# Softmax and V product of each pair of heads moved ahead of the next pair's key transposes

## Chip, cores and metric

The kernel runs on one core of a Trainium2 chip. The metric is device time in microseconds (us), the median of several executions. Before the change it is 446.15 us, the median of three (444.69 to 447.6). The profiled execution took 449.3 us, and its span from first to last instruction is 447.5 us.

## What is computed

One decoding step of a transformer block: batch 8, one new token, width 1024. Attention has 32 query heads on 4 key/value heads, a cache of 8192 keys, heads of width 128. A ReGLU block with 3584 hidden units follows, and both blocks take shift, scale and gate from a conditioning vector.

```python
mod = (_silu(c) @ w_mod)            # six parts: sa, ca, ga, sb, cb, gb
h = _layernorm(x) * (1 + ca) + sa
q = (h @ wq).reshape(B, Sq, Hq, Dh)          # 8, 1, 32, 128
scores = einsum('bhqd,bhkd->bhqk', q, k) * Dh ** (-0.5)   # 8192 keys
p = softmax(scores)
o = einsum('bhqk,bhkd->bhqd', p, v)
x = x + ga * (o @ wo)
h = _layernorm(x) * (1 + cb) + sb
x = x + gb * (relu(h @ W_gate) * (h @ W_up)) @ W_down
```

Nearly all bytes are the two caches: 8 batches x 4 key/value heads x 8192 x 128 x 2 bytes, 67 MB each. With the weights the profile counts 185.6 MB read from the chip's memory.

## The kernel before

The 32 (batch, key/value head) items are taken two at a time, so the attention loop runs over `M = 16` pairs m (L495). A pair needs one 4 MB key load and one 4 MB value load. Everything that is streamed goes through one ring in the on-chip memory, `arena`: nine slots of 8192 bf16 per partition. A key or value load fills two slots, so in the steady state four loads fit: K(m+2) overwrites K(m), and V(m+2) overwrites V(m) (because K(4) no longer fits at the end and wraps to the start).

All loads are issued by one engine, SyncE (SP), in one order: K(0), V(0), K(1), V(1), ..., then Wo, gate, up and down (L223 to L259). SyncE waits before each one until the last reader of the bytes it overwrites is through, and a load that waits holds back all later ones. The readers are the eight key transposes of the pair (`kt_part`, L423, on VectorE), and its 32 V products (`pv`, L477, on TensorE). After the attention the ring goes on with the weights: the second half of gate (gate 1) overwrites the first half of Wo.

Work on the compute engines stands in the order in which it is written; semaphores are planned from reads and writes (`Prog.plan`). For each pair:

- `kt_part(m, e8)`, e8 = 0..7: VectorE transposes an eighth of the keys, as 32-bit words, into a ring of six buffers `kt`.
- `qk_part(m, e8)`: four matmuls on TensorE (L434) for each eighth. The first four eighths go to one bank of PSUM, the other four to a second.
- `rowmax(m, h)`: VectorE takes the negated maximum of a bank (L441). `spread` joins the two on VectorE (L445) and spreads them over the partitions with a matmul (L447).
- `headmax`: two small VectorE operations (L452, L455) give the bias of the exponential.
- `expo`: ScalarE takes the exponential of both banks (L461), with the row sums.
- `p_turn`: two VectorE transposes of the probabilities (L468).
- `pv`: 32 matmuls (L477) that sum into bank 5.
- `fold`: four VectorE operations out of bank 5 (L484, L487), then a small matmul (L490).
- `make_qpad(m+2)`: GpSimd places the queries of a later pair (L416).

The order before is a software pipeline: the key work of pair m carries the softmax of pair m-1. After eighth 0 come `rowmax(m-1, 1)` and `spread(m-1)`, after eighth 1 `headmax` and `expo`, after eighth 3 `p_turn`, after eighth 4 `pv`, after eighth 7 `fold`, all of pair m-1. The last pair's softmax follows the loop by itself.

Of the kernel before, what the change touches and what calls it, by code (L numbers as in the profile page):

```python
# [132 lines left out]
def bass_adaLN_cond__gqa_block_cached__glu_gated_reglu__decode_kernel(nc, A_x, A_k_cache, A_v_cache, A_wq, A_wo, B_x, B_W_gate, B_W_up, B_W_down, c, w_mod, out):  # L133
# [18 lines left out]
    with ExitStack() as es:  # L152
# [29 lines left out]
        M = N // 2  # L182
# [24 lines left out]
        def R(t, lo=0, hi=1):  # L207
            return (t, lo, hi)

        def bank(b, n=1):  # L210
            return ("ps", b, b + n)

        def slot_r(lo, hi):
            return ("arena", lo, hi)
# [197 lines left out]
        def make_qpad(m):  # L412
            if m >= M:
                return
            for Q in range(4):
                P.op("pool", lambda e, n=2 * m + Q // 2, Q=Q: e.tensor_copy(  # L416
                    qpad[32 * Q:32 * Q + 32, m % 2, :, 24 + 32 * Q:32 + 32 * Q], qR[32 * Q:32 * Q + 32, :, n, :]),
                     reads=[R("qR", 0, 8)], writes=[R("qpad", m % 2, m % 2 + 1)])

        def kt_part(m, e8):  # L420
            lo = place["k", m] + e8 * QE
            to = (8 * m + e8) % 6 * QE
            P.op("dve", lambda e: e.transpose(ktb[:, to:to + QE].bitcast(dt.uint32), arena[:, lo:lo + QE].bitcast(dt.uint32)),  # L423
                 reads=[slot_r(lo, lo + QE)], writes=[R("kt", to, to + QE)])

        def qk_part(m, e8):
            to = (8 * m + e8) % 6 * QE
            i = e8 % 4
            b = 2 * (m % 2) + e8 // 4
            kv = ktb[:, to:to + QE].rearrange("p (c t k r) -> p c t k r", t=2, k=32, r=2)  # L430
            fns = []
            for t in range(2):
                for r in range(2):
                    fns.append(lambda e, t=t, r=r: e.matmul(  # L434
                        ps[:, b, :].rearrange("p (c k) -> p c k", k=32), qpad[:, m % 2, t * 2 + r, 24 - 8 * i:152 - 8 * i],
                        kv[:, :, t, :, r], start=(i == 0 and t == 0 and r == 0), stop=(i == 3 and t == 1 and r == 1)))
            P.op("pe", fns, reads=[R("kt", to, to + QE), R("qpad", m % 2, m % 2 + 1)], writes=[bank(b)])

        def rowmax(m, h):
            b = 2 * (m % 2) + h  # L440
            P.op("dve", lambda e: e.tensor_reduce(negm[:, h:h + 1], ps[:, b, :], AX.X, ALU.max, negate=True),  # L441
                 reads=[bank(b)], writes=[R("negm", h, h + 1)])

        def spread(m):
            P.op("dve", lambda e: e.tensor_tensor(out=negm[:, 2:3], in0=negm[:, 0:1], in1=negm[:, 1:2], op=ALU.min),  # L445
                 reads=[R("negm", 0, 2)], writes=[R("negm", 2, 3)])
            P.op("pe", lambda e: e.matmul(ps[:, 4, 0:128], negm[:, 2:3].to_broadcast([128, 128]), identf[:],  # L447
                                         start=True, stop=True), reads=[R("negm", 2, 3), R("identf")], writes=[bank(4)])

        def headmax(m):  # L450
            z = m % 2
            P.op("dve", lambda e: e.tensor_reduce(mj[:].rearrange("p (g j) -> p g j", g=2),  # L452
                                                  ps[:, 4, 0:128].rearrange("p (g m j) -> p g j m", g=2, j=J), AX.X, ALU.min),
                 reads=[bank(4)], writes=[R("mj")])
            P.op("dve", lambda e: e.scalar_tensor_tensor(out=mjt[:], in0=mj[:], scalar=1.0, in1=jms[:], op0=ALU.mult,  # L455
                                                         op1=ALU.mult, accum_out=bias[:, z:z + 1]),
                 reads=[R("mj"), R("jms")], writes=[R("mjt"), R("bias", z, z + 1)])

        def expo(m):
            z = m % 2  # L460
            P.op("act", lambda e: e.activation(prb[:], ps[:, 2 * z:2 * z + 2, :].rearrange("p h n -> p (h n)"), ACT.Exp,  # L461
                                               bias=bias[:, z:z + 1], scale=scale, accum_out=lall[:, m:m + 1]),
                 reads=[bank(2 * z, 2), R("bias", z, z + 1)], writes=[R("prb"), R("lall", m, m + 1)])

        def p_turn(m):
            z = m % 2
            for g in range(2):
                P.op("dve", lambda e, g=g: e.transpose(pT[64 * g:64 * g + 64, z, :, g, :], prb[64 * g:64 * g + 64, :]),  # L468
                     reads=[R("prb"), R("pT", z, z + 1)], writes=[R("pT", z, z + 1)])

        def pv(m):
            z = m % 2
            lo = place["v", m]
            vv = arena[:, lo:lo + 2 * SLOT].rearrange("p (h i c d) -> p h c i d", h=2, i=4, d=Dh)
            fns = []
            for t in range(32):
                fns.append(lambda e, t=t: e.matmul(  # L477
                    ps[64 * (t % 2):64 * (t % 2) + 64, 5, :].rearrange("p (i d) -> p i d", d=Dh),
                    pT[:, z, t].rearrange("p g x -> p (g x)"), vv[:, t // 16, t % 16], start=(t < 2), stop=(t >= 30),
                    tile_position=(0, 64 * (t % 2))))  # L480
            P.op("pe", fns, reads=[slot_r(lo, lo + 2 * SLOT), R("pT", z, z + 1)], writes=[bank(5)])

        def fold(m):
            P.op("dve", lambda e: e.tensor_scalar(out=om[:], in0=ps[:, 5, 0:Dh], scalar1=im[:, 0:1], scalar2=None, op0=ALU.mult),  # L484
                 reads=[bank(5), R("im")], writes=[R("om")])
            for i in range(1, 4):
                P.op("dve", lambda e, i=i: e.scalar_tensor_tensor(  # L487
                    out=om[:], in0=ps[:, 5, Dh * i:Dh * i + Dh], scalar=im[:, i:i + 1], in1=om[:], op0=ALU.mult, op1=ALU.add),
                     reads=[bank(5), R("im"), R("om")], writes=[R("om")])
            P.op("pe", lambda e: e.matmul(ps[:, 6, 16 * m:16 * m + 16], om[:], jmp[:].rearrange("p g j -> p (g j)"),  # L490
                                         start=True, stop=True), reads=[R("om"), R("jmp")], writes=[bank(6)])

# [2 lines left out]
        for m in range(M):  # L495
            for e8 in range(8):
                kt_part(m, e8)
                qk_part(m, e8)
                if m >= 1:
                    if e8 == 0:  # L500
                        rowmax(m - 1, 1)
                        spread(m - 1)
                    elif e8 == 1:
                        headmax(m - 1)
                        expo(m - 1)
                    elif e8 == 3:
                        p_turn(m - 1)
                    elif e8 == 4:
                        pv(m - 1)
                    elif e8 == 7:  # L510
                        fold(m - 1)
                if e8 == 5:
                    rowmax(m, 0)
            make_qpad(m + 2)
        rowmax(M - 1, 1)
        spread(M - 1)
        headmax(M - 1)
        expo(M - 1)
        p_turn(M - 1)
        pv(M - 1)  # L520
        fold(M - 1)


        P.op("dve", lambda e: e.tensor_tensor(out=lx[:], in0=lall[:, :, None].to_broadcast([128, M, 2 * J]),
# [127 lines left out]
```

## Time and profile before

| | |
|---|---|
| Median of three | 446.15 us (444.69 to 447.6) |
| Span of the profiled execution | 447.5 us |
| TensorE matmul busy | 267.8 us, 60% |
| VectorE busy | 262.7 us, 59% |
| ScalarE busy | 28.8 us, 6% |
| Main DMA queue, share of 16 engines' span | 97.7% |
| Read from memory | 185.63 MB, 415 GB/s over the span |
| 128 key transposes (L423) | 1224 ns each |
| 32 probability transposes (L468) | 1220 ns each |
| V products, 32 of a pair (L477) | 3.64 to 6.36 us a pair |
| Key landings that VectorE waits for | 55.9 us in 16 waits |

A page of this kind divides the span into 40 slices and gives each engine's busy share there, the clock that TensorE was granted, and the rate of the DMA engines. A window view does the same for any stretch of time. The chain view follows the end of the kernel back through what each step waited for. The timeline lists instructions in order of start, with the idle time before each and what ended it.

A compute engine at 60% and a DMA queue at 98% mean that the bytes are the first limit. What the order of the compute instructions can still change is when a slot of the ring comes free, and so whether the DMA engines have anything to fetch.

### The profile page before, as it was taken

The numbers are of one execution on the slowest core, as the hardware profiler recorded it, in microseconds if no ns is written. First come the engines' busy times: TensorE is split into PE (matmuls) and PEld (weight loads), VectorE is DVE, ScalarE is ACT, GpSimd is POOL, SyncE is SP. The second block draws the span as 40 slices with busy tenths as digits, with TensorE's granted clock in tenths as the row PEclk, the third lists the DMA queues.
The fourth block names the chain that finished last, engine by engine and source line by source line (L and its number), as shares of the span: only waits on it lengthen the run. The fifth ranks groups of instructions, "written<-read, shape, count | busy, mean of one in ns | idle before, by whom it ended". The sixth has DMA issues, their size and how long they took to land.

```text
span 447.5 us, 4025 instructions
## 1 busy us (share of the span) xinstructions
PE 267.8 (60%) x1690; PEld 114.4 (26%) x1690; DVE 262.7 (59%) x371; ACT 28.8 (6%) x48; POOL 19.9 (4%) x77
## 2 busy tenths in 40 slices
PE   0244335565687756586777757566777758535435
PEld 0111011132223323232323313222323323224212
DVE  0503054679596967869586866949596866353020
ACT  0200001101011010101011010101011010110000
POOL 6000010000000000000000000000000000000000
PEclk9986559598969989689888988998889988668855
DMA  8999999999999999999999999999899999999995
GB/s 348 415 435 425 447 434 429 428 431 436 429 431 404 435 451 422 425 414 428 425 432 387 428 423 390 425 425 438 363 442 377 439 425 420 440 418 396 419 427 212
DMA packets 7554, 185.90 MB, mean 415 GB/s; under 512 B 912, under 2 KB 1008, under 8 KB 1264
## 3 DMA queue, kind: packets, MB, share of 16 engines
q1 hardware_dynamic: 7504, 185.64, 97.7%
q8 instruction: 13, 0.21, 0.2%
q14 instruction: 5, 0.04, 0.0%
q10 hardware_dynamic: 32, 0.01, 0.0%
HBM read 185.63 MB, written 0.02 MB: 415 GB/s over the span
## 4 chain that ended last, share of the span: by engine, by line
DMA 45%; PE 25%; DVE 24%; issue 5%; ACT 1%; SPq 0%; POOL 0%; DVEq 0%; ACTq 0%; POOLq 0%
DMA arena<-in_A_k_cache_dram 37%; DVE kt L423 12%; PE ps L477 11%; PE ps L434 8%; DVE pT L468 6%; DMA arena<-in_B_W_down_dram 6%; DMA c_r<-in_c_dram 2%; PE ps L562 1%; PE ps L347 1%; PE ps L583 1%; DVE negm L441 1%; DVE mj L452 1%; PE ps L447 1%; DVE mjt L455 0%; DVE kt L552 0%
## 5 line engine op out<-in xcount | busy, mean ns | idle before, releaser
L434 PE MATMUL ps<-kt,qpad 128*128 128x512 bf16 x512 | 148.1, 430 | 105.1 <-DVE kt L423 61.8
L423 DVE STREAM_TRANSPOSE kt<-arena 128x1024 uint32<-128x1024 uint32 x128 | 152.8, 1224 | 56.3 <-DMA arena<-in_A_k_cache_dram 55.9
L434 PEld LDWEIGHTS ps<-kt,qpad 128*128 128x128 bf16 x512 | 47.4, 105 | 189.1 <-DVE kt L423 89.1
L477 PE MATMUL ps<-arena,pT 128*64 128x512 bf16 x512 | 72.5, 447 | 4.5 <-DVE pT L468 4.5
L477 PEld LDWEIGHTS ps<-arena,pT 128*64 128x64 bf16 x512 | 32.6, 128 | 44.8 <-issue 28.6
L468 DVE STREAM_TRANSPOSE pT<-prb 64x1024 bf16<-64x1024 bf16 x32 | 39.0, 1220 | 1.8 <-ACT prb L461 1.3
L461 ACT ACTIVATE prb<-ps,bias 128x1024 bf16<-128x1024 f32 x16 | 17.8, 1113 | 289.2 <-DVE mjt L455 289.2
L416 POOL COPY qpad<-qR 32x32 bf16<-32x32 bf16 x64 | 13.0, 203 | 321.8 <-PE ps L434 269.2
L484 DVE TENSOR_SCALAR om<-ps,im 128x128 f32<-128x128 f32 x16 | 5.6, 351 | 32.1 <-PE ps L477 32.1
L441 DVE TENSOR_REDUCE negm<-ps 128x1 f32<-128x512 f32 x32 | 20.9, 653 | 1.2 <-PE ps L434 1.2
L487 DVE SCALAR_TENSOR_TENSOR om<-ps,im,om 128x128 f32<-128x128 f32 x48 | 16.8, 351 | 1.7
L583 PE MATMUL ps<-arena,hT 128*32 128x448 bf16 x128 | 9.3, 457 | 10.1 <-DMA arena<-in_B_W_up_dram 6.8
L370 PE MATMUL ps<-arena,hT 128*32 128x512 bf16 x64 | 6.7, 566 | 12.2 <-DMA arena<-in_A_wq_dram 9.3
L347 PE MATMUL ps<-arena,hT 128*32 128x512 bf16 x96 | 9.7, 574 | 5.7 <-DMA arena<-in_w_mod_dram 5.7
L316 PE MATMUL ps<-st,sel 128*128 128x1 f32 x4 | 1.0, 311 | 19.6 <-DVE st L315 19.6
L601 PE MATMUL ps<-arena,kt 128*32 128x256 bf16 x112 | 6.9, 416 | 7.4 <-DMA arena<-in_B_W_down_dram 7.3
L590 DVE TENSOR_TENSOR kt<-ps,kt 128x448 bf16<-128x448 f32 x2 | 1.2, 620 | 17.3 <-PE ps L583 17.3
L354 DVE COPY mod<-ps 128x512 f32<-128x512 f32 x2 | 1.3, 670 | 14.7 <-PE ps L347 14.7
L380 DVE CAST kt<-ps 128x512 bf16<-128x512 f32 x1 | 0.7, 691 | 15.4 <-PE ps L370 15.4
L447 PEld LDWEIGHTS ps<-identf,negm 128*128 128x128 f32 x32 | 8.2, 266 | 5.3 <-DVE negm L445 2.3
L447 PE MATMUL ps<-identf,negm 128*128 128x128 f32 x32 | 8.4, 356 | 0.9 <-DVE negm L445 0.9
L288 DVE TENSOR_SCALAR lt<-lt 128x256 f32<-128x256 f32 x1 | 0.3, 293 | 13.3 <-ACT lt L287 13.3
(77 smaller groups left out, 94.9 us busy)
## 6 DMA issues: line engine op xcount, KB each, us to landing
arena<-in_A_k_cache_dram SPq DMA_DIRECT2D x16, 4096.0 KB, 24.3
arena<-in_A_v_cache_dram SPq DMA_DIRECT2D x16, 4096.0 KB, 14.8
arena<-in_w_mod_dram SPq DMA_DIRECT2D x4, 3072.0 KB, 14.7
arena<-in_A_wq_dram SPq DMA_DIRECT2D x4, 2048.0 KB, 29.6
arena<-in_A_wo_dram SPq DMA_DIRECT2D x2, 4096.0 KB, 25.0
arena<-in_B_W_gate_dram SPq DMA_DIRECT2D x2, 3584.0 KB
arena<-in_B_W_up_dram SPq DMA_DIRECT2D x2, 3584.0 KB
arena<-in_B_W_down_dram SPq DMA_DIRECT2D x1, 3584.0 KB
```

Of the source, the lines that this page charges most:

```text
L347: fns.append(lambda e, w=w, pr=pr, j=j, kk=kk: e.matmul(ps[32 * j:32 * j + 32, pr, :], hT[:, kk, :], w[:, 2 * pr:2 * pr + 2, j, :], start= ...
L416: P.op("pool", lambda e, n=2 * m + Q // 2, Q=Q: e.tensor_copy(qpad[32 * Q:32 * Q + 32, m % 2, :, 24 + 32 * Q:32 + 32 * Q], qR[32 * Q:32 * ...
L423: P.op("dve", lambda e: e.transpose(ktb[:, to:to + QE].bitcast(dt.uint32), arena[:, lo:lo + QE].bitcast(dt.uint32)), reads=[slot_r(lo, lo ...
L434: fns.append(lambda e, t=t, r=r: e.matmul(ps[:, b, :].rearrange("p (c k) -> p c k", k=32), qpad[:, m % 2, t * 2 + r, 24 - 8 * i:152 - 8 * ...
L441: P.op("dve", lambda e: e.tensor_reduce(negm[:, h:h + 1], ps[:, b, :], AX.X, ALU.max, negate=True), reads=[bank(b)], writes=[R("negm", h, ...
L447: P.op("pe", lambda e: e.matmul(ps[:, 4, 0:128], negm[:, 2:3].to_broadcast([128, 128]), identf[:], start=True, stop=True), reads=[R("negm" ...
L461: P.op("act", lambda e: e.activation(prb[:], ps[:, 2 * z:2 * z + 2, :].rearrange("p h n -> p (h n)"), ACT.Exp, bias=bias[:, z:z + 1], scal ...
L468: P.op("dve", lambda e, g=g: e.transpose(pT[64 * g:64 * g + 64, z, :, g, :], prb[64 * g:64 * g + 64, :]), reads=[R("prb"), R("pT", z, z + ...
L477: fns.append(lambda e, t=t: e.matmul(ps[64 * (t % 2):64 * (t % 2) + 64, 5, :].rearrange("p (i d) -> p i d", d=Dh), pT[:, z, t].rearrange(" ...
L487: P.op("dve", lambda e, i=i: e.scalar_tensor_tensor(out=om[:], in0=ps[:, 5, Dh * i:Dh * i + Dh], scalar=im[:, i:i + 1], in1=om[:], op0=ALU ...
L583: fns.append(lambda e, w=w, r=kk - r0, kk=kk, h=h, j=j, b0=b0: e.matmul(ps[32 * j:32 * j + 32, b0 + h, 0:H], hT[:, kk, :], w[:, r, j, h, : ...
L601: fns.append(lambda e, w=w, r=k - r0, k=k, j=j: e.matmul(ps[32 * j:32 * j + 32, 4, 0:256], hmT[:, k, :], w[:, r, j, :], start=(k == 0), st ...
```

## The change

The softmax of a pair no longer rides in the next pair's key work. After the eight eighths of pair m come its `rowmax(m, 1)`, `spread`, `headmax`, `expo`, `p_turn` and `pv`, and only then the first key transpose of pair m+1. The purpose is to have each pair's value slots read, and so released, before the next pair starts. `fold` of the pair before is placed where VectorE would otherwise wait for the last scores, and its matmul is split off as `fold_pe`, behind `spread`. No operation is added or removed, and the instructions themselves stay as they are.

```diff
@@ -487,6 +487,8 @@
                 P.op("dve", lambda e, i=i: e.scalar_tensor_tensor(
                     out=om[:], in0=ps[:, 5, Dh * i:Dh * i + Dh], scalar=im[:, i:i + 1], in1=om[:], op0=ALU.mult, op1=ALU.add),
                      reads=[bank(5), R("im"), R("om")], writes=[R("om")])
+
+        def fold_pe(m):
             P.op("pe", lambda e: e.matmul(ps[:, 6, 16 * m:16 * m + 16], om[:], jmp[:].rearrange("p g j -> p (g j)"),
                                          start=True, stop=True), reads=[R("om"), R("jmp")], writes=[bank(6)])
 
@@ -496,29 +498,21 @@
             for e8 in range(8):
                 kt_part(m, e8)
                 qk_part(m, e8)
-                if m >= 1:
-                    if e8 == 0:
-                        rowmax(m - 1, 1)
-                        spread(m - 1)
-                    elif e8 == 1:
-                        headmax(m - 1)
-                        expo(m - 1)
-                    elif e8 == 3:
-                        p_turn(m - 1)
-                    elif e8 == 4:
-                        pv(m - 1)
-                    elif e8 == 7:
-                        fold(m - 1)
                 if e8 == 5:
                     rowmax(m, 0)
             make_qpad(m + 2)
-        rowmax(M - 1, 1)
-        spread(M - 1)
-        headmax(M - 1)
-        expo(M - 1)
-        p_turn(M - 1)
-        pv(M - 1)
+            if m >= 1:
+                fold(m - 1)
+            rowmax(m, 1)
+            spread(m)
+            if m >= 1:
+                fold_pe(m - 1)
+            headmax(m)
+            expo(m)
+            p_turn(m)
+            pv(m)
         fold(M - 1)
+        fold_pe(M - 1)
```

## The prediction

> **What bounds the kernel now.** I read the page first: the slices of the DMA, then the chain.
>
> ```profile
> DMA  8999999999999999999999999999899999999995
> GB/s 348 415 435 425 447 434 429 428 431 436 429 431 404 435 451 422 425 414 428 425 432 387 428 423 390 425 425 438 363 442 377 439 425 420 440 418 396 419 427 212
> DMA 45%; PE 25%; DVE 24%; issue 5%; ACT 1%; SPq 0%; POOL 0%; DVEq 0%; ACTq 0%; POOLq 0%
> ```
>
> The DMA engines count as busy from start to end, so the bytes are the limit. But the rate isn't even: from the twenty-second slice on, some slices fall to 387, 390, 363, 377. The chain, less than half DMA, says that compute has a say in the loads. So I asked for the rate by stage, and for single microseconds around a dip (columns: stretch, its length, busy us of PE, PEld, DVE, ACT and POOL, granted clock, DMA share, GB/s).
>
> ```profile
> 62.50:160.00 97.50, 63.60 (x304) 25.72 (x304) 69.02 (x89) 6.10 (x9) 4.05 (x20) 0.85 1.00 428
> 160.00:200.00 40.00, 28.44 (x136) 11.84 (x136) 29.73 (x41) 2.41 (x4) 1.47 (x8) 0.83 1.01 432
> 200.00:240.00 40.00, 28.43 (x136) 11.82 (x136) 29.71 (x41) 2.41 (x4) 1.78 (x9) 0.87 0.99 418
> 240.00:280.00 40.00, 28.08 (x136) 11.91 (x136) 29.60 (x40) 2.41 (x4) 0.81 (x4) 0.87 0.97 410
> 280.00:360.00 80.00, 54.72 (x273) 22.66 (x273) 59.28 (x80) 4.82 (x8) 3.25 (x16) 0.89 0.98 416
> 361.60:441.00 79.40, 43.74 (x482) 22.87 (x482) 32.40 (x50) 5.47 (x9) 0.00 (x0) 0.71 0.99 419
> 317.00:318.00 1.00, 1.00 (x11) 0.38 (x8) 0.00 (x0) 0.00 (x0) 0.00 (x0) 1.00 0.46 197
> 318.00:319.00 1.00, 1.00 (x7) 0.46 (x6) 0.85 (x3) 0.00 (x0) 0.00 (x0) 1.00 0.08 33
> ```
>
> Undisturbed, the stream runs at 428 to 432 GB/s; later it runs at 415, and at 318 us it nearly stops. What it waited for stands in the waits of SyncE's queue and in the timelines around another dip.
>
> ```profile
> SPq L235 <- PE ps L477: 248.8, 13, 21.9
> ```
>
> ```profile
> 271.93 5.33 PE L477 MATMUL ps<-arena,pT 128*64 128x512 bf16 x32
> ```
>
> ```profile
> 277.30 0.33 SPq L235 DMA_DIRECT2D arena<-in_A_v_cache_dram  x1
> 277.67 0.43 SPq L235 DMA_DIRECT2D arena<-in_A_k_cache_dram  x1
> 280.17 1.25 DVE L423 STREAM_TRANSPOSE kt<-arena 128x1024 uint32<-128x1024 uint32 x1 [1.35 <-DMA arena<-in_A_k_cache_dram]
> ```
>
> SyncE stands behind the V products (L477). When they end at 277.26, V and K are issued together, and the previous K load, the last one in flight, lands only 2.9 us later. [...] So the queue holds under 1 us of data when it is refilled, or none: it runs by a hair, and dry whenever the V products are late.
>
> How late they are follows the pair's key landing T. With V products of 3.64 us the issue comes at T + 14.7 (landing at 239.85, issue at 254.59); with 5.33 us at T + 16.5 (260.76 to 277.30, 301.53 to 318.07, 322.42 to 338.90). The key landings are 19.4 to 21.4 us apart, 19.9 on average (62.69 to 361.61 over 15).
>
> [...] V products take 3.64 us at full clock and 6.36 in the tail at a clock near 0.5.
>
> **The change, part by part.** Nothing is removed or added; the same 128 transposes, 1024 large matmuls and 16 exponentials run. What moves:
>
> *Exposed softmax.* Pair 15 has no next pair to ride in, so the tail of before already shows the new order:
>
> ```profile
> 380.09 0.69 DVE L441 TENSOR_REDUCE negm<-ps 128x1 f32<-128x512 f32 x1 [1.19 <-PE ps L434]
> 381.03 0.49 PE L447 MATMUL ps<-identf,negm 128*128 128x128 f32 x2 [0.85 <-DVE negm L445]
> 382.10 1.11 ACT L461 ACTIVATE prb<-ps,bias 128x1024 bf16<-128x1024 f32 x1 [15.69 <-DVE mjt L455]
> 383.34 2.51 DVE L468 STREAM_TRANSPOSE pT<-prb 64x1024 bf16<-64x1024 bf16 x2 [1.27 <-ACT prb L461]
> 386.00 6.36 PE L477 MATMUL ps<-arena,pT 128*64 128x512 bf16 x32 [4.48 <-DVE pT L468]
> 392.40 0.35 DVE L484 TENSOR_SCALAR om<-ps,im 128x128 f32<-128x128 f32 x1 [6.54 <-PE ps L477]
> ```
>
> From the second rowmax to the end of the probability transposes: 380.09 to 385.85, 5.76 us, of which VectorE is idle about 2 us (spread and exponential). These 2 us are the added waits; queued behind them are the next pair's key transposes, and TensorE waits for those. From a key landing the VectorE path is: six transposes 6.88 (timeline at 62.69), first rowmax 0.65, two more transposes 2.37, fold 1.49 (which covers the wait for the last scores, 1.04 us at full clock), then 5.76: 17.15 us. The keys come every 19.5 us at 430 GB/s (8.39 MB). VectorE still ends 2.4 us before the next landing: the added waits lie beside the transfer and cost nothing.
>
> *TensorE.* The V products now stand ahead of the next pair's scores. Its first rowmax needs four eighths of scores. Counted from the end of the probability transposes: V products done at 0.15 + 5.33 = 5.5, and 16 score matmuls back to back take 3.7 (12 take 2.78 at 254.48), so 9.2. VectorE reaches that rowmax at 2.4 + 6.88 = 9.3. Even; no stall. If keys were always there, the period would be 9.2 + 0.65 + 2.37 + 1.49 + 5.76 = 19.5, as long as the transfer. With 3.64 us of V products it is 17.8; with 6.36 us and the first four scores at half clock (1.86 us, as at 221.03) 11.2 + 10.3 = 21.5. That last value is the unknown. One gap of some 4 us per pair remains on TensorE instead of two, and the scores keep it busy after it; I take 5.33.
>
> *The release.* The key slots are read at T + 6.88 + 0.65 + 2.37 = T + 9.9, and K(m+2) may be issued then. V products end at T + 17.15 + 0.15 + 5.33 = T + 22.6, and V(m+2) follows. At that moment the queue holds the rest of V(m+1), which lands at T + 29.3 (6.7 us), and all of K(m+2) (9.75 us): 16 us of data where it was under 1. Even half-clock V products can't empty it.
>
> *What it brings.* From 200 to 360 us the rate rises from 415 (418, 410, 416 weighted) to 430: 160 x (1 - 415/430) = 5.6 us. In the tail the attention ends earlier after the last key landing (17.15 + 5.5 = 22.6 us, where it was 392.40 - 361.61 = 30.8), so the weights' slots come free earlier. That is worth 0 to 2.0 us (79.4 us at 419 against 430); I take 0, because only two windows of the tail dip. `fold_pe` stands in TensorE's gap and hides beside the exponential. Span: 5.6 us less. But the profiled run is 3.15 us slower than the median (449.3 against 446.15), and I can't say how much of that is dips. I take 0.5 us off: 5.1 us, so 446.15 - 5.1 = 441.0 us.
>
> **The rivals.**
> 1. *The dips are mostly the profile's* (no change): if all 3.15 us of excess were dips, unprofiled runs lose 2.5 us, which gives 443.7; if none of the low rate is starvation, 446. For it: some slices of low rate have a DMA share near 1. Against: the windows at 317 and 318 us coincide to the microsecond with late V products.
> 2. *TensorE or VectorE becomes the bound* (slower): if half of the pairs have the period of 21.5 and half 19.2, the mean is 20.3 against 19.9, 15 x 0.4 = 6 us more: 452. For it: the period with keys always there is within 0.1 us of the transfer. Against: [...] 16 us of queue absorb single late pairs.
> 3. *More gain*: the tail and the first half also rise, to the 432 GB/s seen: 5.6 + 2 + 1 = 8.6 us, 437.5.
>
> **How the numbers follow.** Forecast 0.52, rival 1 0.28, rival 2 0.10, rival 3 0.10. One per cent is 4.46 us, so faster means below 441.7: the forecast lies on that line's good side by little, and part of it counts as no change. Faster 0.56, same 0.34, slower 0.10. The range goes from rival 3 to the near end of rival 1: 437.5 to 444.5.
>
> **What would show it.** Right: K landings 19.4 to 19.7 us apart throughout; V issues at T + 22 to 23, K issues at T + 10; no window of 1 us under 300 GB/s between 62 us and the end of the keys; VectorE still idle for the keys, 1 to 3 us a pair. Wrong: VectorE's wait ahead of L423 gone or given to TensorE (rival 2), or V issued early and the rate still 415 (rival 1).

## The result, and the profile after

The changed kernel takes 441.1 us (median of four, 440.45 to 441.2), the kernel before 446.88 us with one more execution beside it (444.69 to 452.79). The ratio is 0.9884, 95% interval 0.9842 to 0.9925: faster by 1.2%. The ratio leaves out the 452.79 us, which counts as a slow execution. The span of the profiled execution falls from 447.5 to 439.3 us. The kernel before also spreads widely from one execution to the next, over 8 us; the changed one stays within 0.75 us. In the later experiments the kernel before had medians of 450.2 to 450.4 us, so against those the gain is some 9 us.

From the page of the changed kernel, the slices of the DMA rate, the chain that ended last, and two groups (busy us, mean ns, then the idle time before it and what ended most of it):

```profile
GB/s 345 423 427 428 449 433 431 430 433 431 430 433 433 428 433 433 435 433 439 436 431 433 433 428 430 433 430 431 433 437 427 445 430 431 423 436 406 435 416 200
PE 42%; DVE 33%; DMA 16%; ACT 5%; issue 2%; SPq 0%; POOL 0%; DVEq 0%; ACTq 0%; POOLq 0%
L423 DVE STREAM_TRANSPOSE kt<-arena 128x1024 uint32<-128x1024 uint32 x128 | 147.8, 1211 | 12.0 <-DMA arena<-in_A_k_cache_dram 11.7
L441 DVE TENSOR_REDUCE negm<-ps 128x1 f32<-128x512 f32 x32 | 22.0, 686 | 37.8 <-PE ps L434 37.8
```

The dips of the rate are gone: no slice after the first is under 423 until the weights at the end. But the chain changed the other way. DMA is now 16% of it and TensorE 42%, and VectorE waits 11.7 us for keys where it waited 55.9. By the chain alone one would call this kernel bound by compute. The windows show where the bytes went (columns as in the prediction):

```profile
62.50:160.00 97.50, 66.17 (x308) 28.59 (x310) 73.00 (x96) 7.31 (x11) 4.06 (x20) 0.83 1.00 432
200.00:240.00 40.00, 28.14 (x144) 12.73 (x146) 31.32 (x43) 2.41 (x4) 1.62 (x8) 0.84 1.01 433
240.00:280.00 40.00, 28.46 (x138) 12.65 (x136) 29.38 (x41) 2.41 (x4) 1.62 (x8) 0.84 1.00 432
350.00:433.00 83.00, 45.94 (x491) 24.29 (x488) 34.13 (x55) 5.47 (x9) 0.00 (x0) 0.75 1.00 426
```

The stages that ran at 418 and 410 GB/s run at 433 and 432. One pair on the timeline of the changed kernel:

```profile
218.94 6.88 DVE L423 STREAM_TRANSPOSE kt<-arena 128x1024 uint32<-128x1024 uint32 x6
219.06 5.81 PE L477 MATMUL ps<-arena,pT 128*64 128x512 bf16 x32 [4.35 <-DVE pT L468]
224.90 0.33 SPq L235 DMA_DIRECT2D arena<-in_A_v_cache_dram  x1
228.48 0.69 DVE L441 TENSOR_REDUCE negm<-ps 128x1 f32<-128x512 f32 x1 [2.67 <-PE ps L434]
231.48 0.33 SPq L235 DMA_DIRECT2D arena<-in_A_k_cache_dram  x1
235.99 2.51 DVE L468 STREAM_TRANSPOSE pT<-prb 64x1024 bf16<-64x1024 bf16 x2 [1.27 <-ACT prb L461]
```

V and K are no longer issued together into an empty queue, but 6.6 us apart. VectorE starts the keys at once (they are there), and then stands 2.67 us at the first rowmax, because TensorE did the V products first.

The end moved too. SyncE's timeline of the kernel before shows the issue of gate 1, which waits for the Wo products and so for the attention:

```profile
404.94 0.33 SPq L235 DMA_DIRECT2D arena<-in_B_W_gate_dram  x1
```

and the same line of the changed kernel:

```profile
397.10 0.33 SPq L235 DMA_DIRECT2D arena<-in_B_W_gate_dram  x1
```

From there to the end of the span are 42.6 us before and 42.2 us after. The last pair's keys also start earlier. Before:

```profile
361.61 1.25 DVE L423 STREAM_TRANSPOSE kt<-arena 128x1024 uint32<-128x1024 uint32 x1 [3.89 <-DMA arena<-in_A_k_cache_dram]
```

and after:

```profile
357.56 6.88 DVE L423 STREAM_TRANSPOSE kt<-arena 128x1024 uint32<-128x1024 uint32 x6
```

So of the 7.8 us by which gate 1 goes out earlier, 4.0 come from the earlier start of the last keys and 3.8 from the shorter way from there (39.5 us, before 43.3).

### The profile page after: what moved, and what is told of

Read it like the earlier page. It is cut to its first block, busy times and chain, and to the rows that moved or that the text cites. A ratio compares the mean times of both kernels' runs of the same rounds, so it can differ in the third digit from the quotient of the medians.

```text
span 439.3 us, 4039 instructions
## 1 busy us (share of the span) xinstructions
PE 271.2 (62%) x1690; PEld 121.7 (28%) x1690; DVE 263.0 (60%) x371; ACT 28.8 (7%) x48; POOL 20.0 (5%) x77
## 4 chain that ended last, share of the span: by engine, by line
PE 42%; DVE 33%; DMA 16%; ACT 5%; issue 2%; SPq 0%; POOL 0%; DVEq 0%; ACTq 0%; POOLq 0%
PE ps L477 22%; PE ps L434 14%; DVE pT L468 9%; DMA arena<-in_A_k_cache_dram 9%; DVE kt L423 9%; DMA arena<-in_B_W_down_dram 5%; DVE negm L441 5%; ACT prb L461 4%; DVE om L487 4%; DMA c_r<-in_c_dram 2%; PE ps L447 2%; PE ps L556 1%; PE ps L347 1%; DVE mj L452 1%; PE ps L577 1%
## 5 line engine op out<-in xcount | busy, mean ns | idle before, releaser
L423 DVE STREAM_TRANSPOSE kt<-arena 128x1024 uint32<-128x1024 uint32 x128 | 147.8, 1211 | 12.0 <-DMA arena<-in_A_k_cache_dram 11.7
L477 PE MATMUL ps<-arena,pT 128*64 128x512 bf16 x512 | 96.6, 560 | 69.7 <-DVE pT L468 69.7
L434 PE MATMUL ps<-kt,qpad 128*128 128x512 bf16 x512 | 121.9, 384 | 11.1 <-DVE kt L423 9.8
L477 PEld LDWEIGHTS ps<-arena,pT 128*64 128x64 bf16 x512 | 46.1, 159 | 114.1 <-issue 109.9
L434 PEld LDWEIGHTS ps<-kt,qpad 128*128 128x128 bf16 x512 | 45.8, 97 | 85.7 <-DVE kt L423 27.6
L441 DVE TENSOR_REDUCE negm<-ps 128x1 f32<-128x512 f32 x32 | 22.0, 686 | 37.8 <-PE ps L434 37.8
L447 PEld LDWEIGHTS ps<-identf,negm 128*128 128x128 f32 x32 | 4.7, 186 | 26.0 <-DVE negm L445 24.5
L452 DVE TENSOR_REDUCE mj<-ps 128x16 f32<-128x128 f32 x16 | 4.7, 291 | 9.3 <-PE ps L447 9.3
```

The costliest lines, as they stand in the source:

```text
L434: fns.append(lambda e, t=t, r=r: e.matmul(ps[:, b, :].rearrange("p (c k) -> p c k", k=32), qpad[:, m % 2, t * 2 + r, 24 - 8 * i:152 - 8 * ...
L477: fns.append(lambda e, t=t: e.matmul(ps[64 * (t % 2):64 * (t % 2) + 64, 5, :].rearrange("p (i d) -> p i d", d=Dh), pT[:, z, t].rearrange(" ...
```

## The experiments

My theory: the gain is the early release of the value slots, which keeps the queue full, and nothing else; the changed kernel runs at the time of the byte stream. Rivals: the order of the compute work or the shorter end of the attention gives the gain; or the compute path, which fills the chain after, sets its time. "Before beside it" is the kernel before, in the same session.

### Releasing the value slot late, first attempt

```diff
-            P.op("pe", fns, reads=[slot_r(lo, lo + 2 * SLOT), ...
+            P.op("pe", fns[:16], reads=[slot_r(lo, last), ...
+            let_go(m - 1)          # in the other run: ahead of pv(m)
+            P.op("pe", fns[16:], reads=[slot_r(lo, last), ...
```

> The changed kernel, in which the slot of V(m) is let go only in the middle of the V products of pair m+1: one small matmul there reads the slot's last column, and the products of pair m are no longer counted as its last reader (m up to 13). Order of all other work unchanged. Theory (the gain comes from the early release of the value slots): the release moves to about T + 20.5 us after a key landing T. Before, two loads issued into a dry queue landed 24 us after the issue (277.30 to 301.53, 318.07 to 341.97), so two pairs take 20.5 + 24 us, 22.2 us a pair against 19.8: about 13 x 2.4 = 31 us more, 472 us, with DMA gaps in every pair. Rival (the gain comes from the order of the compute work or the shorter tail): 441 to 443 us, since the compute order is the same.

> As the run with the late release, but the small matmul stands just ahead of the V products of pair m+1, at about T + 15.3 us, near where the order of before released (14.7 to 16.5). Theory with (release + 24)/2: 19.65 us a pair, at the edge between transfer and compute: 441 to 445 us, with dips in the DMA rate like those of before. Rival (compute order or tail): 441 us and no dips.

Measured: 707.02 and 697.27 us (before beside them 450.31). Neither theory says that, and the edit was at fault. The recorder (`Prog`, which turns the written order into waits and places the loads) queues a load as soon as every part of its slot has had one reader. Where nothing held a column back at that moment, the first half of the split products was that reader, and the load was queued ahead of the second half, which then waited for it. The second half in turn counted as a reader of the new bytes. So from pair 4 on V(m+2) was queued ahead of the whole V product of pair m, which waited for it and read the new values. On the late-front kernel's timeline of TensorE:

```profile
315.28 5.11 PE L477 MATMUL ps<-arena,pT 128*64 128x512 bf16 x32 [19.67 <-DMA arena<-in_A_v_cache_dram]
```

TensorE stands about 19 us for V in each pair, and a pair takes 33.7 us (315.28 to 348.96). These two runs tell nothing of the release, only what a pair costs when its loads and its compute take turns.

### Releasing the value slot late, in three doses

V products in one piece again. A small matmul, put later, is the last column's only counted reader:

```diff
+        def let_go(m, z):
+            if 0 <= m < M - 2:
+                end = place["v", m] + 2 * SLOT
+                P.op("pe", lambda e: e.matmul(..., arena[:, end - 1:end], ...), reads=[slot_r(end - 1, end), ...])
...
             p_turn(m)
+            let_go(m - 1, m % 2)   # 15: free; 17: reads pT too; 23: behind pv(m)
             pv(m)
```

> The changed kernel, V products in one piece; the last column of V(m)'s slot counts as read only by a small added matmul just ahead of the V products of pair m+1, about 15.3 us after a key landing T (m up to 13). All else in place. Theory: K(m+3) and V(m+2) are then issued into a dry queue and K lands 24 us later, so two pairs take 15.3 + 24 us, 19.65 a pair; the first load still early. Last key landing at 63.6 + 15 x 19.65 to 19.8 = 358 to 361, then 81 us of weights and 6 us of end: 445 to 448 us, dips in the DMA rate as in the kernel before. Rival (order of compute or tail brings the gain): 441 us.

> The same, but the small matmul also reads the pair's transposed probabilities, so that it waits for their end, about T + 17.3 us. Theory: (17.3 + 24)/2 = 20.65 us a pair over 12 pairs, 19.8 over 3: last key landing at 371, 456 to 459 us. Rival: 441 us.

> The same, the small matmul behind the V products of pair m+1, about T + 22.9 us. Theory: (22.9 + 24)/2 = 23.4 us a pair: last key landing at 404, 488 to 492 us. Rival: 441 us.

| kernel | release after a key landing, intended | expected us | measured us | ratio to before |
|---|---|---|---|---|
| changed | at the pair's own V products | | 441.1 | 0.9884 |
| late15 | T + 15.3 | 445 to 448 | 444.76 | 0.9901 (0.987 to 0.9932) |
| late17 | T + 17.3 | 456 to 459 | 454.68 | 1.0123 (1.0072 to 1.0174) |
| late23 | T + 22.9 | 488 to 492 | 483.41 | 1.0768 (1.071 to 1.0825) |

From the timelines of late17, its loads and the landing they lead to:

```profile
224.00 6.88 DVE L423 STREAM_TRANSPOSE kt<-arena 128x1024 uint32<-128x1024 uint32 x6 [4.26 <-DMA arena<-in_A_k_cache_dram]
241.07 0.33 SPq L235 DMA_DIRECT2D arena<-in_A_v_cache_dram  x1
264.63 6.88 DVE L423 STREAM_TRANSPOSE kt<-arena 128x1024 uint32<-128x1024 uint32 x6 [2.87 <-DMA arena<-in_A_k_cache_dram]
```

Keys land at 224.00, both loads go out 17.07 us later, and the keys of two pairs on land 23.6 us after that. Eleven pairs from 140.18 to 367.07 take 20.63 us each; the formula gave 20.65. With the compute order of the changed kernel untouched, the release alone moves the time over 42 us. That is shown.

The changed kernel's ratio is from the first session; against the 450.44 beside the late kernels, 441.1 is 0.979. The releases themselves lay 14.9, 17.4 and 23.2 us after a landing, on the average of the twelve held-back loads. All three times came out below their ranges, by 0.2, 1.3 and 4.6 us. The largest dose is off most: 22.8 us a pair (140.16 to 390.94 over 11) against 23.4. There the loads landed 21.8 to 23.0 us after their issue (256.56 to 278.32, 211.19 to 234.15), so the 24 us in the formula was too much.

The smallest dose says one thing more. It releases about as late as the kernel before (14.9 us after a landing, before 15.6), and still it takes 444.76 us where before beside it took 450.44. Its dips are shallower than expected, 422 to 430 GB/s by stage from 160 to 360 us where before had 410 to 432. By the formula the 0.7 us between the two releases are worth (15.6 - 14.9)/2 x 12 = 4 us, an estimate; the shorter end of the attention, which this kernel keeps, is the other candidate. No run tells the two apart.

### Does the compute path of the changed kernel cost anything?

The first run here puts idle matmuls into an unused bank in the gap ahead of the V products, to keep the clock up; the second leaves 28 of the 32 V products out.

```diff
             p_turn(m)
+            P.op("pe", [lambda e: e.matmul(ps[:, 7, :], identb[:], ...)] * 16, ...)
             pv(m)
```

```diff
-            for t in range(32):
+            for t in (0, 1, 30, 31):
```

> The changed kernel with 16 idle matmuls (128 x 512, into an unused bank) in TensorE's gap ahead of each pair's V products, so that the clock stays full and the V products take 3.64 us where they take 4.95 to 6.58. Theory (the time is set by the DMA stream, and the compute path, although it now fills the chain, only eats into the queue): 440.5 to 441.2 us, no change; VectorE waits for keys again by 1 to 2 us a pair. Rival (the compute path, 42% TensorE in the chain, sets the time): the period falls from 19.8 to 19.4 us at best by the keys or 17.8 by compute, so 435 to 437 us.

> The changed kernel with 4 of each pair's 32 V products left out of none but kept alone: t = 0, 1, 30, 31 run, the other 28 are left out, so most of the V work is missing and the rest stands. Theory (the changed kernel runs at the stream's own time): 440.5 to 441.2 us, no gain from 5 us less TensorE work a pair. Rival (the compute path still costs something): under 439 us.

Measured: 441.22 us with the idle matmuls, 440.79 us with most V products left out. From the page of the first, the chain and the groups of the key transposes and the V products:

```profile
DMA 76%; DVE 19%; PE 3%; SPq 1%; issue 0%; ACT 0%; POOL 0%; POOLq 0%
L423 DVE STREAM_TRANSPOSE kt<-arena 128x1024 uint32<-128x1024 uint32 x128 | 147.6, 1210 | 45.7 <-DMA arena<-in_A_k_cache_dram 45.7
L477 PE MATMUL ps<-arena,pT 128*64 128x512 bf16 x512 | 58.3, 380 | 14.3 <-DVE pT L468 14.3
```

V products now take 3.64 us a pair (58.3 over 16) at a granted clock of 1.00 where it was 0.84 (160 to 200 us), TensorE is 3% of the chain instead of 42%, VectorE waits 45.7 us for keys again, and gate 1 is issued at 388.69, 8.4 us earlier. The time is the same. The chain of the changed kernel followed a path that had fallen behind inside the reserve, and the stream was just as long. That the stream sets the time of the changed kernel is shown: with most V products left out, 0.3 us are gained.

### Where the fold stands

```diff
-            if m >= 1:
-                fold(m - 1)
             rowmax(m, 1)
             spread(m)
-            if m >= 1:
-                fold_pe(m - 1)
             headmax(m)
             expo(m)
             p_turn(m)
+            if m >= 1:
+                fold(m - 1)
+                fold_pe(m - 1)
             pv(m)
```

> One part of the change undone: fold of the pair before and its matmul stand behind the probability transposes, not in the wait for the last scores. The V products must then wait for fold to empty bank 5. Theory: 1.5 us more per pair on the path, 0.16 us less at the second rowmax, so a period of 21.1 to 21.3 us; that is over the transfer's 19.4, the queue's reserve of 16 us is eaten up and the rest shows: the attention ends some 22 us later, 460 to 466 us. Rival (the reserve hides it): under 445 us.

> The kernel with the late fold (458.7 us), with 24 idle matmuls behind each pair's spread, so that its V products run at full clock. Theory (the late fold cost time only because a period of 21.3 us is over the transfer's 19.4): 3.64 us of V products instead of 5 to 6.6 and scores without a stall give 19.3 us: 441 to 443 us. Rival (the fold ahead of the V products costs its 1.5 us a pair whatever the rest): 455 us or more.

Measured: 458.66 us for the late fold (ratio 1.0214, 1.0156 to 1.0272), and 441.25 us for the same order with 24 idle matmuls behind `expo`. Of the late fold, the page's DMA rate and two successive spreads on the timeline:

```profile
GB/s 347 428 425 428 440 433 431 439 430 434 433 433 430 428 436 431 440 427 436 430 397 436 384 418 380 441 378 403 418 324 449 361 427 377 429 344 287 435 406 206
```

```profile
222.31 0.16 DVE L445 TENSOR_TENSOR negm<-negm 128x1 f32<-128x1 f32 x1
243.65 0.16 DVE L445 TENSOR_TENSOR negm<-negm 128x1 f32<-128x1 f32 x1
```

The period is 21.3 us here and 21.1 on average (V products starting at 81.18 and 398.03, over 15), the low end of what was expected, and over the transfer's 19.4. For the first twenty slices this costs nothing: the reserve pays. Then the rate breaks up. The loss, 17.6 us over the changed kernel, is a little under the 19 us expected at least. With the idle matmuls the granted clock is 1.00 from 160 to 350 us, where the late fold has 0.79 to 0.83. All sixteen pairs have V products of 3.64 us, 19.54 us apart (81.21 to 374.26 over 15), and the same order costs nothing.

### Could the old order have had the gain?

The V products an eighth earlier in the kernel before; idle matmuls in TensorE's gaps of the kernel before; and both.

```diff
-                    elif e8 == 3:
+                    elif e8 == 2:
                         p_turn(m - 1)
-                    elif e8 == 4:
+                    elif e8 == 3:
                         pv(m - 1)
```

```diff
                         p_turn(m - 1)
+                        P.op("pe", [... ps[:, 7, :] ...] * 11, ...)
...
             make_qpad(m + 2)
+            P.op("pe", [... ps[:, 7, :] ...] * 10, ...)
...
         p_turn(M - 1)
+        P.op("pe", [... ps[:, 7, :] ...] * 16, ...)
```

> The kernel before, with its pipelined order kept, but the transposes of the probabilities after eighth 2 (were: 3) and the V products after eighth 3 (were: 4). Theory: the V products end, and the loads are issued, at T + 13.3 (full clock) to 15.0 us where it was 14.7 to 16.5; (14 + 24)/2 = 19.0 us a pair is below the transfer's 19.4, so the dips go: 441.5 to 443 us. Rival (the gain needs the new order, with the whole softmax ahead of the keys): within 1 us of the kernel before.

> The kernel before, order kept, with idle matmuls (128 x 512, unused bank) in TensorE's gaps: 11 ahead of eighth 4's scores, 10 at the end of each pair, 16 in the last softmax. No work moved. Theory (before, the V products at half clock made the loads late and the end of the attention late): V products of 3.64 us, loads issued at T + 14.7, (14.7 + 24)/2 = 19.35 us a pair, under the transfer's 19.4; attention ends earlier, and the stream sets the time: 441 to 442.5 us. Rival (only the new order gives the gain): 446 to 450 us.

> The same idle matmuls, with the V products also one eighth earlier than in the kernel before. Theory: loads at T + 13.3, stream-bound: 441 to 441.5 us, as the changed kernel. Rival: as the kernel with the earlier V products alone, 448 to 449 us.

Measured: 448.82 us with the earlier V products (before beside it 450.44, ratio 0.9978, 0.9943 to 1.0012), 441.35 us with the idle matmuls alone (before beside it 450.24, ratio 0.9791), 441.08 us with both.

The first is a miss. The V products did move, but took 4.7 us on average where they took 4.5, so the loads went out only 0.7 us earlier (14.9 against 15.6 us after a landing, means over the pairs). From 200 to 360 us the rate rose to 427 to 430 GB/s, but it still dipped earlier (414 from 160 to 200 us). The last keys landed at 360.15 instead of 361.61. Then the end gave it back, as its timeline shows:

```profile
371.27 5.55 PE L477 MATMUL ps<-arena,pT 128*64 128x512 bf16 x32
376.75 3.65 PE L434 MATMUL ps<-kt,qpad 128*128 128x512 bf16 x16
380.44 0.69 DVE L441 TENSOR_REDUCE negm<-ps 128x1 f32<-128x512 f32 x1 [2.06 <-PE ps L434]
405.46 0.33 SPq L235 DMA_DIRECT2D arena<-in_B_W_gate_dram  x1
```

The V products of pair 14 now stand ahead of sixteen of the last pair's score matmuls instead of twelve. The last rowmax begins at 380.44 (380.09 before), gate 1 goes out at 405.46 (404.94 before), and the span is 447.4 us.

The second shows that the gain does not need the new order. No work moved, and 9 us are gone. Two landings and the issue between them, from its timelines:

```profile
199.37 1.25 DVE L423 STREAM_TRANSPOSE kt<-arena 128x1024 uint32<-128x1024 uint32 x1 [3.57 <-DMA arena<-in_A_k_cache_dram]
213.59 0.33 SPq L235 DMA_DIRECT2D arena<-in_A_v_cache_dram  x1
218.72 1.25 DVE L423 STREAM_TRANSPOSE kt<-arena 128x1024 uint32<-128x1024 uint32 x1 [3.61 <-DMA arena<-in_A_k_cache_dram]
```

All sixteen pairs have V products of 3.64 us; the granted clock is 0.92 to 1.00 by stage from 62 to 350 us, where from 62 to 360 us it was 0.83 to 0.89. The loads go out 14.2 us after a landing, 5.1 us before the next one, and the keys come 19.35 us apart here, 19.5 on average. At the dips of before they went out 2.9 to 4.4 us ahead (277.30 to 280.17, 318.07 to 322.42). So the old order was not too late by its nature, but by its clock: in the kernel before, the granted clock was 0.67 or 0.68 over the five V products of 5.27 to 5.33 us (at 210.47, 230.85, 271.93, 312.70 and 333.59), and 1.00 over those of 3.64 us at 93.20, 151.25, 250.91 and 352.52. This run doesn't separate the release from the end of the attention either: the last softmax has idle matmuls too. The last keys start at 355.26, 6.4 us earlier than before, and gate 1 follows after 40.4 us instead of 43.3.

### Two limits, side by side

From each kernel's profile, the issue of gate 1 and what follows it:

| kernel | gate 1 issued | to the end of the span | span |
|---|---|---|---|
| before | 404.94 | 42.6 | 447.5 |
| before, V earlier | 405.46 | 41.9 | 447.4 |
| late fold | 415.28 | 42.1 | 457.4 |
| changed | 397.10 | 42.2 | 439.3 |
| before, idle matmuls | 395.62 | 44.3 | 439.9 |
| changed, idle matmuls | 388.69 | 50.5 | 439.2 |
| 28 V products left out | 386.25 | 52.4 | 438.6 |

Where the attention ends late, the end follows 42 us later. Where it ends early, the stream's own 439 us stand. The changed kernel lies where the two meet: by these numbers a microsecond more at gate 1 would show, which no run tested.

The kernels with a late release are not in the table, because their stream had lost time before: gate 1 goes out at 396.32, 402.99 and 425.77, and 45.6, 49.7 and 55.1 us follow.

The kernel before is near both limits, and the change moved both. By the sums below, its stream was some 6.4 us behind by 360 us (6.3 + 1.0 - 0.9). So, as an estimate, a shorter end with the old dips would have left a span of some 446 us. A full queue with the old way of 43.3 us to gate 1 would have left 441 to 443 (last keys at 355.3 to 357.6, and 42.2 us behind gate 1). My theory that the early release is the gain and nothing else is therefore too strong: the release is the larger part, and the shorter end is needed for the rest. No run changed the end alone.

## Why the prediction was right

The time was forecast at 441.0 us and measured at 441.1, inside the range, and the likeliest case came true. By its steps:

- *The bound.* Right. The dips were an empty queue (33 GB/s from 318 to 319 us, behind the issue at 318.07), and the time after is the stream's: two kernels with less on the compute path are within 0.3 us of it. That the queue of before held under 1 us of data when it was refilled was my estimate; measured are the 2.87 us from the issue at 277.30 to the landing at 280.17.
- *The refilled rate.* I took 430 GB/s, from the 428 to 432 of the undisturbed stages of before, and that was nearly it: 432 or 433 GB/s in every stage of the changed kernel from 62 to 350 us, at most 435 in any refilled one (the changed kernel with idle matmuls, 160 to 200 us). No run shows what keeps it from going higher.
- *Exposed softmax.* Sized at 5.76 us; on the timeline of the changed kernel it runs from 213.16 to 218.91, 5.75 us. It lies beside the transfer, as said.
- *TensorE: "Even; no stall".* This step failed. I took 5.33 us of V products; they took 4.92 to 6.58, at granted clocks from 0.73 down to 0.54, and 6.04 on average (96.6 us over 16). VectorE waits 37.8 us for scores ahead of the rowmaxes, nearly all of it ahead of the first of a pair, where I expected none. The period became 19.79 us (V products starting at 81.10 and 377.93, over 15), longer than the transfer's 19.4. So the premise of rival 2 held in kind, compute sets the pace of the pairs, and its time did not: the period is 19.79 us and not 20.3, under the 19.9 of before, and the excess over the transfer, 15 x 0.4 = 6 us, came out of the reserve. The sign that I named, VectorE waiting 1 to 3 us a pair for keys, was there only up to 160 us.
- *The release.* Right in kind, and too large. K is issued 11.7 us after the start of the keys (200.21 to 211.88), which is T + 9.9 plus a stall of 1.8. V is issued 25.5 us after the start of its pair's keys (179.85 to 205.30), not at T + 22.6. So less is left in the queue than the 16 us I had: bytes issued and not yet moved, at 432 GB/s, make 13.2 us at 106.40, 11.3 at 224.90 and 8.8 at 343.92. In the late fold the same count falls from 12.5 us at 87.74 to 1.0 at 235.24, and there its rate breaks up. The sign that no microsecond would fall under 300 GB/s came true but for the grain of the count: the lowest up to the end of the keys are 295, nine packets of 32 KB, where before it was 33.
- *What it brings.* Too small, and evened out by chance. Forecast 5.6 us of span, then 5.1; the span fell 8.2. The stages from 200 to 360 us reached 432 and not 430: 160 x (1 - 415/432) = 6.3 us. The stages before gained 1.0. The end, which I took as 0, went from 419 to 426 GB/s: 79.4 x (1 - 419/426) = 1.3 us. The first keys landed 0.9 us later. That is 7.7 of the 8.2. The sum counts bytes and not causes. The 0 for the end was a guess from two dips, and too little: the way from the last keys to gate 1 became 3.8 us shorter.
- *The half microsecond off, for a profile that was slower than the median.* Too small, by as much as the gain was: 8.2 us of span against 446.15 - 441.1 = 5.05 us of median leave 3.15, the whole excess of the profiled execution, where I took 0.5. Two errors of some 2.6 us cancelled, and that is luck. The kernel before isn't steady: 444.69 to 454.47 us over all its executions, which I put down to a queue on the edge of empty. Three early executions gave 446.15. Against 450.2 the gain is 9 us, and the forecast of 5.1 is little more than half of it.

## What to carry to other kernels

In a ring of buffers, compute each load's issue against the landing ahead of it, not only the busy share of the queue: here 98% busy hid 2% of loss and nearly all of the spread from one execution to the next. In a ring that holds two rounds, as here, two loads issued together into a dry queue give a period of (time from landing to release + time from issue to landing)/2; where that passed the transfer time, the release was the bound (late17: 20.65 us by the formula, 20.63 measured, 19.4 for the transfer). Look at the end as well: here the way from the last keys to the first weight load that waits for the attention was nearly a second limit. And the chain of waits doesn't tell a bound from a path that is merely using up slack: taking 5 us of TensorE work a pair away moved a chain with 42% TensorE by 0.3 us.

## What I had not expected

The V products' durations in the changed kernel repeat: 4.95, 5.81, 6.25, 6.46, 6.58 us, and again. From 200.32 on, the granted clock over them is 0.72, 0.62, 0.57, 0.54 and 0.54. The pair that starts at 219.06 stands above; five pairs on:

```profile
318.04 5.81 PE L477 MATMUL ps<-arena,pT 128*64 128x512 bf16 x32 [4.35 <-DVE pT L468]
```

The granted clock over it is 0.62 again, and the five pairs take 98.98 us. The late fold, with another period, repeats after six pairs: its probability transposes start at 161.52 and 287.79, and at 182.10 and 308.38, 126.27 and 126.28 us apart. What makes the durations repeat was not shown.

A gap of 4.35 us stands ahead of these V products, and filling it raised the granted clock from 0.84 to 1.00 (160 to 200 us). But whether filling the gap pays depends on what it feeds: 16 idle matmuls a pair brought nothing in the changed kernel (441.22), and 21 a pair brought 9 us in the kernel before (441.35 against 450.24), as much as the whole reordering.
